# The scores of two jobs in the same columns, attention written as a software pipeline, and more weight buffers, in a two-layer memory-attention and GLU kernel

## Chip, core and metric

The kernel runs on one core of a Trainium2 chip. The metric is the device time of one execution in microseconds (us). Engines are named as in the profile: PE multiplies matrices (PEld is its weight load), DVE and ACT work on vectors, POOL does small things, and the queue of SP issues the loads.

## The reference, cut

Two layers, each an attention block A and a gated feed-forward block B, with the same weights in both layers. A is a recurrence: 64 segments of 32 rows, each preceded by 8 memory rows, which are the first 8 output rows of the segment before.

```python
for s in range(n_seg):                       # 64 segments of 32 rows
    h = concat([mem, x[:, 32*s:32*s+32]])    # 40 rows of 512
    q, k, v = h@Wq, h@Wk, h@Wv               # 32 heads of 128
    p = softmax(where(mask, q@k.T * scale, -1e9))
    o = (p @ v) @ Wo
    mem = o[:, :8]; outs.append(o[:, 8:])
# x = x + A(layernorm(x)); x = x + B(layernorm(x)); the same two again
# B: (sigmoid(x@Wg) * (x@Wu)) @ Wd, inner width 1792
```

## The kernel before

Both layers run interleaved: in step t, job 0 is segment t of layer one and job 1 is segment t-6 of layer two. A step with both jobs has 2 x 40 = 80 columns; 58 of the 70 steps are such. The 32 heads go in groups of 6, 6, 6, 6, 4 and 4. The feed-forward blocks (128 rows each, one for each layer in four steps) are written between the steps. The kernel builder turns the program text into a fixed instruction order for each engine. It may move an instruction ahead of earlier ones when it expects it to be ready first, and text order is its priority. A matmul that waits then holds up the ones behind it: the prediction shows three such waits, of 0.17 to 0.30 us, in front of Q/K matmuls that start only after them.

```python
# first half of a step, for each group g of heads
for u0 in range(0, gsz, 3):                 # units of 3 heads
    # Q and K of 3 heads: 24 matmuls into pj     (L237)
    # ACT copies pj to qku                       (L98)
    # per head one score matmul of 80 columns    (L255)
    nc.tensor.matmul(o_ap, lhsT=qku[:, i, 0, :], rhs=rhs, start=True, stop=True)
for j in jobs:                              # two mask additions (L261)
    nc.vector.tensor_tensor(out=st[pj_, hs], in0=s_all[pj_, hs, L*j:L*j+L], in1=maskb..., op=ALU.add)
# DVE max, subtract; ACT exp; DVE sum, reciprocal, multiply per job (L275)
# PE transposes the probabilities into pt_ps (L287), DVE copies them to ptsb (L99)
# second half, for each group
#   V matmuls (L299), ACT copy; PV matmuls (L305), ACT copy; output projection (L315)
# ... cut ...
self.gpool = ctx.enter_context(tc.tile_pool(name="gp", bufs=2))   # gate and up tiles, 256 KB each
self.dpool = ctx.enter_context(tc.tile_pool(name="dp", bufs=2))   # down tiles, 256 KB each
```

PSUM, the memory that the matmuls write to, has one bank for scores, one for the transposed probabilities, one for PV, one for the projection, one for everything of the feed-forward (`misc`), and three that Q/K and V share (`pj`).

Of the kernel before, what the change touches and what calls it, by code (L numbers as in the profile page):

```python
# [8 lines left out]
BF16 = mybir.dt.bfloat16  # L9
F32 = mybir.dt.float32  # L10
ACTF = mybir.ActivationFunctionType
ALU = mybir.AluOpType
# [3 lines left out]
P = 128  # L16
MEM = 8
SEG = 32
L = MEM + SEG
JOFF = 64  # L20
LW = JOFF + L
# [6 lines left out]
def fview(base, dims):  # L28
    return bass.AP(tensor=base.tensor, offset=base.offset, ap=[tuple(base.ap[0])] + [tuple(d) for d in dims])


class Kern:
# [103 lines left out]
    def _setup_pools(self):  # L136
        ctx, tc, nc = self.ctx, self.tc, self.nc
# [20 lines left out]
        nc.sync.dma_start(out=self.maskb[JOFF:LW, :], in_=self.maskb[0:L, :])  # L158
        self.hT = cpool.tile([P, R, DC, LWP], BF16, name="hT_all")
        nc.vector.memset(self.hT[:], 0.0)  # L160
        self.qku = [cpool.tile([P, 3, 2, P], BF16, name=f"qku{i}") for i in range(3)]
        for t_ in self.qku:
            nc.gpsimd.memset(t_[:], 0.0)
        self.qku_i = 0
# [21 lines left out]
        self.xpool = ctx.enter_context(tc.tile_pool(name="xp", bufs=1))  # L186
        self.bpool = ctx.enter_context(tc.tile_pool(name="bp", bufs=2))
        self.spool = ctx.enter_context(tc.tile_pool(name="sp_small", bufs=4))
        self.gpool = ctx.enter_context(tc.tile_pool(name="gp", bufs=2))
        self.dpool = ctx.enter_context(tc.tile_pool(name="dp", bufs=2))  # L190
        self.oxT = {}
        self.xblk = {}

    def emit_step(self, t):
        nc = self.nc
# [6 lines left out]
        j0 = jobs[0]  # L202
# [10 lines left out]
        def mv(c):  # L213
            if both:
                return fview(hT[:, c, 0:1], [(JOFF, 2), (1, L)])
            return hT[:, c, JOFF * j0:JOFF * j0 + L]
# [1 line left out]
        wo_ps = self.wo_ps  # L218
        first_wo = True
        HGm = self.HG  # L220
        s_all = self.s_ps[:, 0:HGm * 2 * L].rearrange("p (h k) -> p h k", h=HGm)
        pt_all = self.pt_ps[:, 0:HGm * 2 * L].rearrange("p (h k) -> p h k", k=2 * L)
        for g, (h0, gsz) in enumerate(self.groups):
            hs = slice(0, gsz)
            for u0 in range(0, gsz, 3):
                nh = min(3, gsz - u0)
                pq = self.next_pj()
                qku = self.qku[self.qku_i % len(self.qku)]
                self.qku_i += 1
                for i in range(nh):  # L230
                    h = h0 + u0 + i
                    for qk, W in ((0, self.wq), (1, self.wk)):
                        o_ap = pq[:, (2 * i + qk) * ncol:(2 * i + qk + 1) * ncol]
                        if both:
                            o_ap = o_ap.rearrange("p (a b) -> p a b", a=2)
                        for c in range(DC):
                            self.mark("qk_mm", nc.tensor.matmul(o_ap, lhsT=W[:, c, h * P:(h + 1) * P], rhs=mv(c),  # L237
                                                                start=(c == 0), stop=(c == DC - 1)), g)
                src = pq[:, 0:2 * nh * ncol]
                if both:  # L240
                    dst = fview(qku[:, 0, 0, 0:1], [(P, 2 * nh), (JOFF, 2), (1, L)])
                    src = src.rearrange("p (m a b) -> p m a b", a=2, b=L)
                else:
                    dst = fview(qku[:, 0, 0, JOFF * j0:JOFF * j0 + 1], [(P, 2 * nh), (1, L)])
                    src = src.rearrange("p (m b) -> p m b", b=L)
                self.mark("qk_ev", self.evac(dst, src, prefer="act"), g)
                for i in range(nh):
                    hl = u0 + i
                    if both:
                        rhs = fview(qku[:, i, 1, 0:1], [(JOFF, 2), (1, L)])  # L250
                        o_ap = s_all[:, hl, :].rearrange("p (a b) -> p a b", a=2)
                    else:
                        rhs = qku[:, i, 1, JOFF * j0:JOFF * j0 + L]
                        o_ap = s_all[:, hl, L * j0:L * j0 + L]
                    self.mark("s_mm", nc.tensor.matmul(o_ap, lhsT=qku[:, i, 0, :], rhs=rhs, start=True, stop=True), g)  # L255
            st, pb = self.st[g % 2], self.pb[g % 2]
            mx, sm, rs = self.mx[g % 2], self.sm[g % 2], self.rs[g % 2]
            for j in jobs:
                pj_ = slice(0, JOFF) if j == 0 else slice(JOFF, LW)
                npj_ = JOFF if j == 0 else L  # L260
                self.mark("sm_mask", nc.vector.tensor_tensor(  # L261
                    out=st[pj_, hs], in0=s_all[pj_, hs, L * j:L * j + L],
                    in1=self.maskb[pj_, :].unsqueeze(1).to_broadcast([npj_, gsz, L]), op=ALU.add), g)
            self.mark("sm_max", nc.vector.tensor_reduce(out=mx[pr, hs], in_=st[pr, hs], axis=AX.X, op=ALU.max), g)
            self.mark("sm_sub", nc.vector.tensor_tensor(  # L265
                out=st[pr, hs], in0=st[pr, hs],
                in1=mx[pr, hs].unsqueeze(2).to_broadcast([npart, gsz, L]), op=ALU.subtract), g)
            self.mark("sm_exp", nc.scalar.activation(out=st[pr, hs], in_=st[pr, hs], func=ACTF.Exp,  # L268
                                                     scale=self.scale), g)
            self.mark("sm_sum", nc.vector.tensor_reduce(out=sm[pr, hs], in_=st[pr, hs], axis=AX.X, op=ALU.add), g)  # L270
            self.mark("sm_rcp", nc.vector.reciprocal(out=rs[pr, hs], in_=sm[pr, hs]), g)
            for j in jobs:
                pj_ = slice(0, JOFF) if j == 0 else slice(JOFF, LW)
                npj_ = JOFF if j == 0 else L
                self.mark("sm_mul", nc.vector.tensor_tensor(  # L275
                    out=pb[pj_, hs, JOFF * j:JOFF * j + L], in0=st[pj_, hs],
                    in1=rs[pj_, hs].unsqueeze(2).to_broadcast([npj_, gsz, L]), op=ALU.mult), g)
            if both:
                idn = fview(self.ident[:, 0:1], [(JOFF, 2), (1, L)])
            else:  # L280
                idn = self.ident[:, JOFF * j0:JOFF * j0 + L]
            cb = 0 if both else L * j0
            for hl in range(gsz):
                o_ap = pt_all[:, hl, cb:cb + ncol]
                if both:
                    o_ap = o_ap.rearrange("p (a b) -> p a b", a=2)
                self.mark("t_mm", nc.tensor.matmul(o_ap, lhsT=pb[:, hl, :], rhs=idn, start=True, stop=True), g)  # L287
            ptsb = self.ptsb[g]
            self.mark("pt_ev", self.evac(ptsb[:, hs, cb:cb + ncol], pt_all[:, hs, cb:cb + ncol], prefer="dve"), g)
        for g, (h0, gsz) in enumerate(self.groups):  # L290
            vsb = self.vsb[g % 2]
            ptsb = self.ptsb[g]
            hs = slice(0, gsz)
            vun = 3 if gsz % 3 == 0 else 4
            for n in range(gsz // vun):
                pv = self.next_pj()
                col0 = (h0 + vun * n) * P
                for c in range(DC):
                    self.mark("v_mm", nc.tensor.matmul(pv[0:LWP, 0:vun * P], lhsT=hT[:, c, :],  # L299
                                                       rhs=self.wv[:, c, col0:col0 + vun * P],  # L300
                                                       start=(c == 0), stop=(c == DC - 1)), g)
                self.mark("v_ev", self.evac(vsb[pr, vun * n * P:(vun * n + vun) * P], pv[pr, 0:vun * P], prefer="act"), g)
            cb = 0 if both else L * j0
            for hl in range(gsz):
                self.mark("pv_mm", nc.tensor.matmul(  # L305
                    self.ot_ps[:, hl * ncol:(hl + 1) * ncol], lhsT=vsb[:, hl * P:(hl + 1) * P],
                    rhs=ptsb[:, hl, cb:cb + ncol], start=True, stop=True), g)
            otsb = self.otsb[g % 2]
            self.mark("ot_ev", self.evac(otsb[:, hs, 0:ncol],
                                         self.ot_ps[:, 0:gsz * ncol].rearrange("p (h q) -> p h q", q=ncol),  # L310
                                         prefer="act"), g)
            for hl in range(gsz):
                h = h0 + hl
                for c in range(DC):
                    self.mark("wo_mm", nc.tensor.matmul(  # L315
                        wo_ps[:, c * ncol:(c + 1) * ncol], lhsT=self.wo[:, h, c * P:(c + 1) * P],
                        rhs=otsb[:, hl, 0:ncol], start=first_wo, stop=(h == H - 1 and c == DC - 1),
                        skip_group_check=True), g)
                    first_wo = False
        wo3 = wo_ps[:, 0:DC * ncol].rearrange("p (c n) -> p c n", c=DC)  # L320
        nslot = self.hT[:, (t + 1) % R]
        wj = [(idx, j) for idx, j in enumerate(jobs) if (t - j * LAG) + 1 < NSEG]
# [245 lines left out]
```

## Time and profile before

| | before |
|---|---|
| median of 15 runs | 2635.65 us (2632.59 to 2643.47) |
| profiled span, granted clock | 2637.4 us, 0.984 |
| PE busy / streaming at its best | 2276.6 us / 1945 us |
| steps of a block of four | 49.7, 32.9, 36.2, 35.1 us |

"Streaming at its best" is the time that all matmuls would take with no gap between them; the prediction works it out. What the starts hold beyond it is called excess below, and each bit of it is put on the matmul that started late. A step's length is the distance from one copy of the memory rows to the next; the four are averages over the steady part. The lines of the profile stand in the prediction. Line numbers differ between kernels, so each fence below says what is what.

### The profile page before, as it was taken

What the parts mean: (1) busy time and instruction counts of PE and PEld (TensorE: products, weight loads), DVE (VectorE), ACT (ScalarE), POOL (GpSimd) and SP (SyncE); (2) the same over time, 40 slices, a digit from 0 to 9 for tenths busy, and PEclk for the clock granted to TensorE, in tenths of its full rate; (3) what the DMA queues carried; (4) which work ended last, traced back from release to release, by engine and by line L of the source; (5) the groups of instructions that cost most, each with busy time, mean ns of one, the idle gap of its engine ahead of it and who ended that gap; (6) DMA issues with size and microseconds to landing.
All of it is one profiled execution on the core that took longest, in us unless ns stands there. A gap on an engine that the chain in (4) does not pass through costs nothing.

```text
span 2637.4 us, 91952 instructions
## 1 busy us (share of the span) xinstructions
PE 2276.6 (86%) x40820; PEld 1808.3 (69%) x40820; DVE 1463.4 (55%) x4297; ACT 1231.4 (47%) x2829; POOL 50.1 (2%) x94
## 2 busy tenths in 40 slices
PE   5988888888888888888888888888888888888896
PEld 4767676676766667667676767667676776667674
DVE  3545654564565566556555645655565565465452
ACT  2544454444444444444444444444444444444452
POOL 0000000000000000000000000000000000000000
PEclk8999999999999999999999999999999999999997
DMA  8030203132131312213131321313132131313223
GB/s 288 3 88 4 86 18 112 48 90 84 40 108 48 111 48 84 88 38 112 48 112 47 90 85 37 109 48 113 47 89 84 42 102 48 113 44 87 86 59 93
DMA packets 314705, 203.08 MB, mean 77 GB/s; under 512 B 11706, under 2 KB 313794, under 8 KB 314306
## 3 DMA queue, kind: packets, MB, share of 16 engines
q1 hardware_dynamic: 313538, 195.10, 25.1%
q8 instruction: 319, 5.23, 0.8%
q0 software_dynamic: 768, 2.10, 0.2%
q14 instruction: 80, 0.66, 0.1%
HBM read 195.04 MB, written 2.10 MB: 75 GB/s over the span
## 4 chain that ended last, share of the span: by engine, by line
PE 36%; DVE 32%; DMA 15%; ACT 10%; issue 5%; POOL 1%; ACTq 0%; SPq 0%; POOLq 0%; DVEq 0%
PE pj L299 8%; DMA wd<-in_B_w_down_dram 8%; DVE pb L275 7%; PE wo_ps L315 7%; DMA wu<-in_B_w_up_dram 6%; DVE st L261 6%; DVE ptsb L99 5%; PE misc_ps L426 5%; PE pt_ps L287 4%; PE pj L237 3%; ACT qku L98 3%; PE misc_ps L462 3%; ACT vsb L98 3%; DVE sm L270 3%; PE s_ps L255 3%
## 5 line engine op out<-in xcount | busy, mean ns | idle before, releaser
L237 PE MATMUL pj<-hT_all,wk_sb 128*128 128x80 bf16 (+1 forms) x8960 | 690.8, 199 | 0.0
L237 PE MATMUL pj<-hT_all,wq_sb 128*128 128x80 bf16 (+1 forms) x8960 | 662.8, 199 | 12.3 <-DVE hT_all L324 5.7
L299 PE MATMUL pj<-wv_sb,hT_all 128*104 128x384 bf16 (+1 forms) x2800 | 654.6, 344 | 0.0
L98 ACT CAST qku<-pj 128x480 bf16<-128x480 f32 (+1 forms) x840 | 394.9, 483 | 400.0 <-PE pj L237 393.1
L237 PEld LDWEIGHTS <-wq_sb 128*128 128x128 bf16 x8960 | 470.4, 100 | 24.1 <-issue 19.0
L98 ACT CAST vsb<-pj 104x384 bf16<-104x384 f32 (+4 forms) x700 | 347.9, 497 | 288.9 <-PE pj L299 282.5
L237 PEld LDWEIGHTS <-wk_sb 128*128 128x128 bf16 x8960 | 478.8, 100 | 2.2 <-issue 0.6
L315 PEld LDWEIGHTS <-wo_sb 128*128 128x128 bf16 x8960 | 368.9, 99 | 119.8 <-issue 89.6
L315 PE MATMUL wo_ps<-otsb,wo_sb 128*128 128x80 bf16 (+1 forms) x8960 | 397.9, 198 | 19.5 <-ACT otsb L98 13.4
L261 DVE TENSOR_TENSOR st<-s_ps,maskb 64x240 f32<-64x240 f32 (+3 forms) x768 | 287.7, 375 | 193.1 <-PE s_ps L255 176.8
L299 PEld LDWEIGHTS <-hT_all 128*104 128x104 bf16 x2800 | 301.5, 128 | 52.1 <-issue 0.2
L98 ACT CAST otsb<-ot_ps 128x480 bf16<-128x480 f32 (+3 forms) x420 | 202.7, 483 | 201.2 <-PE ot_ps L305 200.2
L275 DVE TENSOR_TENSOR pb<-st,rs 64x240 bf16<-64x240 f32 (+3 forms) x768 | 286.4, 373 | 14.7
L255 PE MATMUL s_ps<-qku 128*128 128x80 bf16 (+1 forms) x2240 | 201.1, 199 | 72.2 <-DVE st L261 37.0
L99 DVE CAST ptsb<-pt_ps 128x480 bf16<-128x480 f32 (+3 forms) x420 | 233.6, 556 | 41.4 <-PE pt_ps L287 32.4
L268 ACT ACTIVATE st<-st 104x240 f32<-104x240 f32 (+5 forms) x420 | 160.5, 382 | 151.9 <-DVE st L265 147.9
L255 PEld LDWEIGHTS <-qku 128*128 128x128 bf16 x2240 | 139.4, 98 | 131.9 <-ACT qku L98 63.0
L305 PEld LDWEIGHTS <-vsb 128*128 128x128 bf16 x2240 | 134.4, 99 | 128.9 <-ACT vsb L98 99.4
L287 PE MATMUL pt_ps<-ident,pb 128*128 128x80 bf16 (+1 forms) x2240 | 148.0, 200 | 73.6 <-DVE pb L275 52.3
L305 PE MATMUL ot_ps<-ptsb,vsb 128*128 128x80 bf16 (+1 forms) x2240 | 190.9, 199 | 21.3 <-ACT vsb L98 12.3
L287 PEld LDWEIGHTS <-pb 128*128 128x128 bf16 x2240 | 100.9, 99 | 133.6 <-DVE pb L275 120.9
L426 PE MATMUL misc_ps<-xnT,wg 128*128 128x128 bf16 x1752 | 171.6, 221 | 23.8 <-DMA wg<-in_B_w_gate_dram 10.0
(70 smaller groups left out, 1684.3 us busy)
## 6 DMA issues: line engine op xcount, KB each, us to landing
wg<-in_B_w_gate_dram SPq DMA_DIRECT2D x224, 256.0 KB, 3.1
wu<-in_B_w_up_dram SPq DMA_DIRECT2D x224, 256.0 KB, 3.7
wd<-in_B_w_down_dram SPq DMA_DIRECT2D x224, 256.0 KB, 2.8
wq_sb<-in_A_Wq_dram SPq DMA_DIRECT2D x4, 768.0 KB, 8.3
wk_sb<-in_A_Wk_dram SPq DMA_DIRECT2D x4, 768.0 KB, 9.2
wv_sb<-in_A_Wv_dram SPq DMA_DIRECT2D x4, 768.0 KB, 11.7
wo_sb<-in_A_Wo_dram SPq DMA_DIRECT2D x4, 768.0 KB, 10.8
x<-in_A_x_dram SPq DMA_DIRECT2D x16, 128.0 KB, 3.4
```

Of the source, the lines that this page charges most:

```text
L98: return nc.scalar.copy(out=out, in_=in_)
L99: return nc.vector.tensor_copy(out=out, in_=in_)
L237: self.mark("qk_mm", nc.tensor.matmul(o_ap, lhsT=W[:, c, h * P:(h + 1) * P], rhs=mv(c), start=(c == 0), stop=(c == DC - 1)), g)
L255: self.mark("s_mm", nc.tensor.matmul(o_ap, lhsT=qku[:, i, 0, :], rhs=rhs, start=True, stop=True), g)
L261: self.mark("sm_mask", nc.vector.tensor_tensor(out=st[pj_, hs], in0=s_all[pj_, hs, L * j:L * j + L], in1=self.maskb[pj_, :].unsqueeze(1).t ...
L268: self.mark("sm_exp", nc.scalar.activation(out=st[pr, hs], in_=st[pr, hs], func=ACTF.Exp, scale=self.scale), g)
L275: self.mark("sm_mul", nc.vector.tensor_tensor(out=pb[pj_, hs, JOFF * j:JOFF * j + L], in0=st[pj_, hs], in1=rs[pj_, hs].unsqueeze(2).to_bro ...
L287: self.mark("t_mm", nc.tensor.matmul(o_ap, lhsT=pb[:, hl, :], rhs=idn, start=True, stop=True), g)
L299: self.mark("v_mm", nc.tensor.matmul(pv[0:LWP, 0:vun * P], lhsT=hT[:, c, :], rhs=self.wv[:, c, col0:col0 + vun * P], start=(c == 0), stop= ...
L305: self.mark("pv_mm", nc.tensor.matmul(self.ot_ps[:, hl * ncol:(hl + 1) * ncol], lhsT=vsb[:, hl * P:(hl + 1) * P], rhs=ptsb[:, hl, cb:cb + ...
L315: self.mark("wo_mm", nc.tensor.matmul(wo_ps[:, c * ncol:(c + 1) * ncol], lhsT=self.wo[:, h, c * P:(c + 1) * P], rhs=otsb[:, hl, 0:ncol], s ...
L426: nc.tensor.matmul(gu[:, 2 * i + k, :], lhsT=W[:, c, i * P:(i + 1) * P], rhs=xnT[:, c, :], start=(c == 0), stop=(c == DC - 1))
```

## The change

Its intent: shorten the softmax chain, keep PE from standing in front of something that has only just been asked for, and let weight loads run further ahead. Cut to its core:

```diff
-        self.qku = [cpool.tile([P, 3, 2, P], BF16, ...
+        self.qku = [cpool.tile([P, 3, 4, P], BF16, ...      # q and k apart for each job, zeros elsewhere
-        ... name="gp", bufs=2     ... name="dp", bufs=2
+        ... name="gp", bufs=3     ... name="dp", bufs=4
-                    nc.tensor.matmul(o_ap, lhsT=qku[:, i, 0, :], rhs=rhs, start=True, stop=True)
+                for idx, j in enumerate(jobs):              # both jobs into the same 40 columns
+                    nc.tensor.matmul(s_all[:, hl, :], lhsT=qku[:, i, j, :],
+                        rhs=qku[:, i, 2 + j, JOFF*j:JOFF*j+L], start=(idx == 0), stop=(idx == len(jobs)-1))
-            for j in jobs: ... tensor_tensor(... maskb ...)
+            one tensor_tensor(... maskb ...) over the rows of both jobs
+        for ui, (g, h0, gsz, u0, nh) in enumerate(units):
+            qku = emit_qk(g, h0, gsz, u0, nh)
+            if pending is not None:
+                emit_scores(...)                             # of the unit before
+                if ...: emit_softmax(...); tps.append((ui + 3, pg, pgsz))
+            while tps and tps[0][0] <= ui: emit_tp(...)      # transposes three units later
+        emit_v(*grp[0])
+        if tps: emit_tp(...)                                 # transposes still to come
+        for k in range(ng):
+            if k + 1 < ng: emit_v(*grp[k + 1])               # V one group ahead
+            if tps: emit_tp(...)
+            emit_pv(*grp[k])
+            if k >= 1: emit_wo(*grp[k - 1])                  # projection one group behind
```

More of the change, by code (lines that the diff above doesn't have):

```diff
@@ L160, in _setup_pools @@
         nc.vector.memset(self.hT[:], 0.0)
-        self.qku = [cpool.tile([P, 3, 2, P], BF16, name=f"qku{i}") for i in range(3)]
+        self.qku = [cpool.tile([P, 3, 4, P], BF16, name=f"qku{i}") for i in range(3)]
         for t_ in self.qku:
@@ L188, in _setup_pools @@
         self.spool = ctx.enter_context(tc.tile_pool(name="sp_small", bufs=4))
-        self.gpool = ctx.enter_context(tc.tile_pool(name="gp", bufs=2))
-        self.dpool = ctx.enter_context(tc.tile_pool(name="dp", bufs=2))
+        self.gpool = ctx.enter_context(tc.tile_pool(name="gp", bufs=3))
+        self.dpool = ctx.enter_context(tc.tile_pool(name="dp", bufs=4))
         self.oxT = {}
@@ L220, in emit_step @@
         HGm = self.HG
-        s_all = self.s_ps[:, 0:HGm * 2 * L].rearrange("p (h k) -> p h k", h=HGm)
+        s_all = self.s_ps[:, 0:HGm * L].rearrange("p (h k) -> p h k", h=HGm)
         pt_all = self.pt_ps[:, 0:HGm * 2 * L].rearrange("p (h k) -> p h k", k=2 * L)
+        units = []
         for g, (h0, gsz) in enumerate(self.groups):
-            hs = slice(0, gsz)
-            for u0 in range(0, gsz, 3):
-                nh = min(3, gsz - u0)
-                pq = self.next_pj()
-                qku = self.qku[self.qku_i % len(self.qku)]
-                self.qku_i += 1
-                for i in range(nh):
-                    h = h0 + u0 + i
-                    for qk, W in ((0, self.wq), (1, self.wk)):
-                        o_ap = pq[:, (2 * i + qk) * ncol:(2 * i + qk + 1) * ncol]
-                        if both:
-                            o_ap = o_ap.rearrange("p (a b) -> p a b", a=2)
-                        for c in range(DC):
-                            self.mark("qk_mm", nc.tensor.matmul(o_ap, lhsT=W[:, c, h * P:(h + 1) * P], rhs=mv(c),
-                                                                start=(c == 0), stop=(c == DC - 1)), g)
-                src = pq[:, 0:2 * nh * ncol]
-                if both:
-                    dst = fview(qku[:, 0, 0, 0:1], [(P, 2 * nh), (JOFF, 2), (1, L)])
-                    src = src.rearrange("p (m a b) -> p m a b", a=2, b=L)
-                else:
-                    dst = fview(qku[:, 0, 0, JOFF * j0:JOFF * j0 + 1], [(P, 2 * nh), (1, L)])
-                    src = src.rearrange("p (m b) -> p m b", b=L)
-                self.mark("qk_ev", self.evac(dst, src, prefer="act"), g)
-                for i in range(nh):
-                    hl = u0 + i
-                    if both:
-                        rhs = fview(qku[:, i, 1, 0:1], [(JOFF, 2), (1, L)])
-                        o_ap = s_all[:, hl, :].rearrange("p (a b) -> p a b", a=2)
-                    else:
-                        rhs = qku[:, i, 1, JOFF * j0:JOFF * j0 + L]
-                        o_ap = s_all[:, hl, L * j0:L * j0 + L]
-                    self.mark("s_mm", nc.tensor.matmul(o_ap, lhsT=qku[:, i, 0, :], rhs=rhs, start=True, stop=True), g)
@@ new lines, in emit_step, with emit_qk @@
+            for u0 in range(0, gsz, 3):
+                units.append((g, h0, gsz, u0, min(3, gsz - u0)))
+        def emit_qk(g, h0, gsz, u0, nh):
+            pq = self.next_pj()
+            qku = self.qku[self.qku_i % len(self.qku)]
+            self.qku_i += 1
+            for i in range(nh):
+                h = h0 + u0 + i
+                for qk, W in ((0, self.wq), (1, self.wk)):
+                    o_ap = pq[:, (2 * i + qk) * ncol:(2 * i + qk + 1) * ncol]
+                    if both:
+                        o_ap = o_ap.rearrange("p (a b) -> p a b", a=2)
+                    for c in range(DC):
+                        self.mark("qk_mm", nc.tensor.matmul(o_ap, lhsT=W[:, c, h * P:(h + 1) * P], rhs=mv(c),
+                                                            start=(c == 0), stop=(c == DC - 1)), g)
+            src = pq[:, 0:2 * nh * ncol]
+            if both:
+                dst = fview(qku[:, 0, 0, 0:1], [(2 * P, 2 * nh), (P + JOFF, 2), (1, L)])
+                src = src.rearrange("p (m a b) -> p m a b", a=2, b=L)
+            else:
+                dst = fview(qku[:, 0, j0, JOFF * j0:JOFF * j0 + 1], [(2 * P, 2 * nh), (1, L)])
+                src = src.rearrange("p (m b) -> p m b", b=L)
+            self.mark("qk_ev", self.evac(dst, src, prefer="act"), g)
+            return qku
@@ L256, in emit_step, with emit_scores, emit_softmax @@
+        def emit_scores(g, u0, nh, qku):
+            for i in range(nh):
+                hl = u0 + i
+                for idx, j in enumerate(jobs):
+                    self.mark("s_mm", nc.tensor.matmul(
+                        s_all[:, hl, :], lhsT=qku[:, i, j, :], rhs=qku[:, i, 2 + j, JOFF * j:JOFF * j + L],
+                        start=(idx == 0), stop=(idx == len(jobs) - 1)), g)
+        def emit_softmax(g, gsz):
+            hs = slice(0, gsz)
             st, pb = self.st[g % 2], self.pb[g % 2]
@@ L257, in emit_step @@
             mx, sm, rs = self.mx[g % 2], self.sm[g % 2], self.rs[g % 2]
-            for j in jobs:
-                pj_ = slice(0, JOFF) if j == 0 else slice(JOFF, LW)
-                npj_ = JOFF if j == 0 else L
-                self.mark("sm_mask", nc.vector.tensor_tensor(
-                    out=st[pj_, hs], in0=s_all[pj_, hs, L * j:L * j + L],
-                    in1=self.maskb[pj_, :].unsqueeze(1).to_broadcast([npj_, gsz, L]), op=ALU.add), g)
+            self.mark("sm_mask", nc.vector.tensor_tensor(
+                out=st[pr, hs], in0=s_all[pr, hs],
+                in1=self.maskb[pr, :].unsqueeze(1).to_broadcast([npart, gsz, L]), op=ALU.add), g)
@@ L277, in emit_step, with emit_tp @@
                     in1=rs[pj_, hs].unsqueeze(2).to_broadcast([npj_, gsz, L]), op=ALU.mult), g)
+        def emit_tp(g, gsz):
+            hs = slice(0, gsz)
+            pb = self.pb[g % 2]
             if both:
@@ L289, in emit_step, with emit_wo, emit_v @@
             self.mark("pt_ev", self.evac(ptsb[:, hs, cb:cb + ncol], pt_all[:, hs, cb:cb + ncol], prefer="dve"), g)
-        for g, (h0, gsz) in enumerate(self.groups):
+        pending = None
+        tps = []
+        for ui, (g, h0, gsz, u0, nh) in enumerate(units):
+            qku = emit_qk(g, h0, gsz, u0, nh)
+            if pending is not None:
+                pg, pgsz, pu0, pnh, pq_ = pending
+                emit_scores(pg, pu0, pnh, pq_)
+                if pu0 + pnh == pgsz:
+                    emit_softmax(pg, pgsz)
+                    tps.append((ui + 3, pg, pgsz))
+            while tps and tps[0][0] <= ui:
+                emit_tp(*tps.pop(0)[1:])
+            pending = (g, gsz, u0, nh, qku)
+        pg, pgsz, pu0, pnh, pq_ = pending
+        emit_scores(pg, pu0, pnh, pq_)
+        emit_softmax(pg, pgsz)
+        tps.append((0, pg, pgsz))
+        def emit_wo(g, h0, gsz):
+            nonlocal first_wo
+            otsb = self.otsb[g % 2]
+            for hl in range(gsz):
+                h = h0 + hl
+                for c in range(DC):
+                    self.mark("wo_mm", nc.tensor.matmul(
+                        wo_ps[:, c * ncol:(c + 1) * ncol], lhsT=self.wo[:, h, c * P:(c + 1) * P],
+                        rhs=otsb[:, hl, 0:ncol], start=first_wo, stop=(h == H - 1 and c == DC - 1),
+                        skip_group_check=True), g)
+                    first_wo = False
+        def emit_v(g, h0, gsz):
             vsb = self.vsb[g % 2]
-            ptsb = self.ptsb[g]
-            hs = slice(0, gsz)
             vun = 3 if gsz % 3 == 0 else 4
@@ L302, in emit_step, with emit_pv @@
                 self.mark("v_ev", self.evac(vsb[pr, vun * n * P:(vun * n + vun) * P], pv[pr, 0:vun * P], prefer="act"), g)
+        def emit_pv(g, h0, gsz):
+            vsb = self.vsb[g % 2]
+            ptsb = self.ptsb[g]
+            hs = slice(0, gsz)
             cb = 0 if both else L * j0
@@ L311, in emit_step @@
                                          prefer="act"), g)
-            for hl in range(gsz):
-                h = h0 + hl
-                for c in range(DC):
-                    self.mark("wo_mm", nc.tensor.matmul(
-                        wo_ps[:, c * ncol:(c + 1) * ncol], lhsT=self.wo[:, h, c * P:(c + 1) * P],
-                        rhs=otsb[:, hl, 0:ncol], start=first_wo, stop=(h == H - 1 and c == DC - 1),
-                        skip_group_check=True), g)
-                    first_wo = False
+        grp = [(g, h0, gsz) for g, (h0, gsz) in enumerate(self.groups)]
+        ng = len(grp)
+        emit_v(*grp[0])
+        if tps:
+            emit_tp(*tps.pop(0)[1:])
+        for k in range(ng):
+            if k + 1 < ng:
+                emit_v(*grp[k + 1])
+            if tps:
+                emit_tp(*tps.pop(0)[1:])
+            emit_pv(*grp[k])
+            if k >= 1:
+                emit_wo(*grp[k - 1])
+        emit_wo(*grp[ng - 1])
         wo3 = wo_ps[:, 0:DC * ncol].rearrange("p (c n) -> p c n", c=DC)
```

## The prediction

> **What bounds the kernel now.** First the page: its engine line, then the chain that ended last.
>
> ```profile
> PE 2276.6 (86%) x40820; PEld 1808.3 (69%) x40820; DVE 1463.4 (55%) x4297; ACT 1231.4 (47%) x2829; POOL 50.1 (2%) x94
> ...
> PE 36%; DVE 32%; DMA 15%; ACT 10%; issue 5%; POOL 1%; ACTq 0%; SPq 0%; POOLq 0%; DVEq 0%
> PE pj L299 8%; DMA wd<-in_B_w_down_dram 8%; DVE pb L275 7%; PE wo_ps L315 7%; DMA wu<-in_B_w_up_dram 6%; DVE st L261 6%; DVE ptsb L99 5%; PE misc_ps L426 5%; PE pt_ps L287 4%; PE pj L237 3%; ACT qku L98 3%; PE misc_ps L462 3%; ACT vsb L98 3%; DVE sm L270 3%; PE s_ps L255 3%
> ```
>
> PE is the fullest engine, yet only 36% of the chain is PE: it keeps being handed to DVE, DMA and ACT. So PE is busy but not streaming. To size that I used the matmul start times in the trace. In the last part of the run, where a step has 40 columns, four matmuls with their weight loads start every 0.10 us (25 ns each); in the middle, with 80 columns, four take 0.14 us (36 ns); eight of 384 columns take 1.48 us with one tail (about 163 ns each). These are max(25, N/2.4 + 2.5) ns. Summed over all recorded matmuls this gives 1945 us of pure streaming. From the first matmul to the last the spacing holds 683 us more than that. I put each excess on the matmul that came late:
>
> - scores (L255) 151; probability transposes (L287) 128; PV (L305) 63; output projection (L315) 68
> - gate/up (L426) 90; down (L462) 85
> - layer-norm transposes (L358) 57; Q, K, V and the rest about 41.
>
> The list of PE's waits names who was late (its figures are smaller, since each break also has a modelled tail of some 0.17 us counted as busy):
>
> ```profile
> PE misc_ps L462 <- DMA wd<-in_B_w_down_dram: 59.0, 89, 3.3
> PE pt_ps L287 <- DVE pb L275: 52.3, 186, 1.2
> PE s_ps L255 <- DVE st L261: 37.0, 134, 0.4
> ...
> PE s_ps L255 <- ACT qku L98: 21.3, 114, 0.4
> PE misc_ps L426 <- DMA wu<-in_B_w_up_dram: 19.5, 37, 1.9
> ```
>
> Then the timeline of one step. The copy of the memory rows into the next step's input (L324) ends a step; here two are 32.9 us apart.
>
> ```profile
> 1230.49 0.22 DVE L324 CAST hT_all<-wo_ps 128x64 bf16<-128x64 f32 x1 [1.33 <-PE wo_ps L315]
> ...
> 1234.97 0.82 DVE L261 TENSOR_TENSOR st<-s_ps,maskb 64x240 f32<-64x240 f32 x2 [1.06 <-PE s_ps L255]
> 1235.83 0.40 DVE L264 TENSOR_REDUCE mx<-st 104x6 f32<-104x240 f32 x1
> ...
> 1255.26 0.49 DVE L99 CAST ptsb<-pt_ps 128x320 bf16<-128x320 f32 x1 [0.41 <-PE pt_ps L287]
> 1263.38 0.22 DVE L324 CAST hT_all<-wo_ps 128x64 bf16<-128x64 f32 x1 [7.64 <-PE wo_ps L315]
> ```
>
> From 1235.0 to 1255.8 DVE works almost without a gap: the six softmax groups set the pace there. Afterwards DVE idles 7.6 us while PE works off V, PV and the output projection. PE's ideal for this step type is 26 us, so 7 us are lost, 4.5 of them in front of scores and transposes. PE's own order in the first half:
>
> ```profile
> 1237.22 0.28 PE L255 MATMUL s_ps<-qku 128*128 128x80 bf16 x3 [0.17 <-ACT qku L98]
> 1238.74 0.27 PE L255 MATMUL s_ps<-qku 128*128 128x80 bf16 x3 [0.20 <-DVE st L261]
> 1239.99 0.39 PE L287 MATMUL pt_ps<-ident,pb 128*128 128x80 bf16 x6 [0.30 <-DVE pb L275]
> ```
>
> Each stands in front of Q/K matmuls that were ready. The instruction order on PE is fixed when the kernel is built, and it puts these a little before their input arrives. Between copies, the four steps of a block last 49.7, 32.9, 36.2 and 35.1 us on average in the steady part (PE ideal 37.0, 26.1, 26.5, 26.8). The long one carries a whole feed-forward block, and its chain alternates between weight load and matmul:
>
> ```profile
> 1212.65 3.49 DMA wd<-in_B_w_down_dram
> 1216.14 0.04 issue
> 1216.18 0.59 PE misc_ps L462 x2
> ...
> 1216.81 3.14 DMA wd<-in_B_w_down_dram
> ```
>
> With two buffers each 256 KB load starts only when an older tile is used up.
>
> **What the Trainium skill says.** "TensorE: Matmul & The Clock Gate", section "Back-to-back issue gap", gives N/2.4 + 2.5 ns for a warm clock and a floor near 25 ns for small N, and warns that weight loads can raise it. The trace agrees with the formula at 80 and 40 columns and shows no weight-load penalty (granted clock 0.984). "PSUM — Partial Sum Buffer", section "PSUM bank collisions raise a hardware error", says writer and reader of one bank must be kept apart; that fits the scores waiting 37.0 us for the mask addition that empties the one score bank. "Perfetto Trace Analysis", section "Identifying Performance Opportunities", says repeated gaps can mean too few buffers; the weight-load chain above is such a case. The same page, section "Optimizing Scalar/DVE Operations", speaks of a fixed cost per DVE instruction and of gain from grouping; here the mask addition takes 395 ns on 64 partitions and 410 on 40, so two cost twice one.
>
> **The change, part by part.**
>
> 1. *Scores of two jobs into the same 40 columns, as two accumulating matmuls.* Steps with both jobs have 1856 score matmuls of 80 columns; they become 3712 of 40: from 36 to 2 x 25 ns each, (50 - 36) x 1856 = +26 us, all on PE. The ACT copy keeps its 480 columns per unit; only its target is spread more widely.
> 2. *One mask addition instead of two.* 768 become 420: 348 fewer at about 375 ns = 130 us less DVE busy time. Per step the starts show 0.43 us for four groups and 0.33 for two, some 2.4 us off the 20.8 us that DVE paces. This is not added to the PE gains; it is one reason for the smaller scores and transposes terms below.
> 3. *Scores one unit later, behind the next unit's Q/K.* 24 matmuls x 36 ns = 0.86 us lie between, against a 0.56 us copy plus latency. The ACT waits should nearly go. Waits for the one score bank shrink but stay, for DVE still paces it. 151 -> 75: -76 us.
> 4. *Transposes three units later.* About 3 us more work ahead of them, but a softmax takes 5 us with its neighbours (1235.0 to 1239.9). The built order still places them by expected readiness. 128 -> 100: -28 us.
> 5. *V of the next group ahead of PV, and the output projection one group later.* V of the next group is 8 x 163 ns = 1.3 us against copies of about 0.5 us, and PV is followed by an older group's 24 x 36 = 0.86 us. PV 63 -> 25, output projection 68 -> 25: -81 us.
> 6. *Three gate/up buffers, four down buffers.* Four of seven down tiles can be resident before they are needed; the rest are asked for earlier. Down 85 -> 40. Gate/up waits also for its one bank and the tanh chain, so 90 -> 65. Together -70 us.
>
> Layer norms and Q/K/V stay at 98. Sum: 26 - 76 - 28 - 81 - 70 = -229 us, or 2637 - 229 = 2408 us. The sizes of the remainders are my choice.
>
> **Rivals.**
>
> *The waits only change place.* DVE still has to finish six softmaxes, and an in-order PE then stands at the transposes instead of the scores. For it: 20.8 us without a gap on DVE, 52 us of waits at transposes. Against: PE's ideal (26 to 37 us a step) is longer than the DVE part even now. Then only the merged mask (up to 2.4 us x 58 steps = 139, half of it hidden) and the loads count, less 26: about 2540.
>
> *The schedule is already as overlapped as this,* and only the extra 26 us of PE and larger strides are felt: 2650. For it: the built order already interleaves V, FFN and Q/K. Against: the 683 us of excess are real gaps.
>
> *The loads are hidden anyway or slow each other,* as three or four in flight share the DMA engines: part 6 gives nothing, 2480. Against: DMA engines are busy some 25% on average.
>
> *Everything overlaps:* DVE no longer paces, excess falls to about 300: 2637 - 683 + 300 + 26 = 2280.
>
> **Range and chances.** Four of the parts pull the same way and only one costs, with a known small cost. The main doubt is how much the DVE rival keeps. I predict 2408 us, with 2290 to 2540 for 8 in 10. Faster by over 2% 0.90, within 2% 0.06, slower by over 2% 0.04.
>
> **What would show it.** Score matmuls near 4096 at 40 columns; mask additions 420 and DVE busy near 1330 us; PE's waits for the qku copy, for vsb and for otsb almost gone; waits at transposes for pb still there; waits for wd at most half of 59 us; ordinary steps near 30 us instead of 33 to 36, and the long one near 45. I am wrong if the transposes' waits grow to what scores, PV and projection lost (first rival), or if DMA keeps its 15% of the chain.

## The result, and the profile after

The median of 8 runs is 2403.35 us (2399.8 to 2409.67). The ratio to the kernel before is 0.9116 (95% interval 0.9103 to 0.9128). A ratio here is the mean time of one kernel's runs over that of the other's in the same rounds, so it isn't quite the ratio of the medians.

The page of the kernel after: engine line and chain.

```profile
PE 2154.7 (90%) x42676; PEld 1830.7 (76%) x42676; DVE 1308.4 (55%) x3949; ACT 1218.4 (51%) x2829; POOL 52.1 (2%) x94
...
PE 41%; DVE 37%; ACT 8%; DMA 6%; issue 5%; SPq 2%; POOL 1%; ACTq 0%; POOLq 0%; DVEq 0%
```

DMA's share of the chain fell from 15% to 6%, ACT's from 10% to 8%. PE has 122 us less busy time although it runs 1856 matmuls more. That is no contradiction: each break in its stream adds a modelled tail, and there are fewer breaks (807 instead of 1465, counted in the two traces). DVE lost 155 us of busy time, most of it the 348 mask additions.

PE's waits in the kernel after (L293 transposes, L509 down, L405 layer-norm transposes, L255 scores):

```profile
PE pt_ps L293 <- DVE pb L277: 60.4, 228, 1.6
PE misc_ps L509 <- DMA wd<-in_B_w_down_dram: 47.2, 49, 2.1
...
PE s_ps L255 <- DVE st L263: 8.7, 50, 0.3
PE s_ps L255 <- ACT qku L98: 8.2, 34, 0.4
```

The two waits of the scores fell from 37.0 and 21.3 us to 8.7 and 8.2. The wait of the transposes for pb rose from 52.3 to 60.4. Gate and up hardly wait for a load any more (0.9 us is left, of 29.5), while the down matmuls still do.

The matching step on DVE (L371 is the copy of the memory rows, L263 the mask addition):

```profile
1116.71 0.23 DVE L371 CAST hT_all<-wo_ps 128x64 bf16<-128x64 f32 x1 [6.95 <-PE wo_ps L321]
...
1122.17 0.41 DVE L263 TENSOR_TENSOR st<-s_ps,maskb 104x240 f32<-104x240 f32 x1 [0.85 <-PE s_ps L255]
...
1139.11 0.49 DVE L99 CAST ptsb<-pt_ps 128x320 bf16<-128x320 f32 x1 [0.41 <-PE pt_ps L293]
1147.38 0.23 DVE L371 CAST hT_all<-wo_ps 128x64 bf16<-128x64 f32 x1 [7.78 <-PE wo_ps L321]
```

The softmax part takes 1139.60 - 1122.17 = 17.4 us instead of 20.8, and the step 30.7 us instead of 32.9. DVE then waits 7.8 us for the projection, much as before.

The excess, worked out as in the prediction, in us:

| in front of | before | after |
|---|---|---|
| scores | 151 | 58 |
| transposes | 128 | 113 |
| PV | 63 | 20 |
| output projection | 68 | 15 |
| gate/up | 90 | 60 |
| down | 85 | 59 |
| layer-norm transposes | 57 | 61 |
| Q, K, V and the rest | 41 | 31 |
| sum | 683 | 417 |
| PE at its best | 1945 | 1971 |

Excess fell by 266 us and the work rose by 26, 240 net, against 238 us between the two profiled spans. A small part of this excess is a slower clock and no wait: the granted clock was 0.984 before and 0.994 after, since the stretches at half clock add up to 85 us before and 30 us after. Some 21 us of the 683 and 8 us of the 417 come from slower matmuls there, an estimate from the starts in these stretches. The steps last 45.1, 30.7, 32.8 and 32.1 us instead of 49.7, 32.9, 36.2 and 35.1.

### The profile page after: what moved, and what is told of

Its sections match the earlier page's. It is cut to its first block, busy times and chain, and to the rows that moved or that the text cites. A ratio compares the mean times of both kernels' runs of the same rounds, so it can differ in the third digit from the quotient of the medians.

```text
span 2399.6 us, 95290 instructions
## 1 busy us (share of the span) xinstructions
PE 2154.7 (90%) x42676; PEld 1830.7 (76%) x42676; DVE 1308.4 (55%) x3949; ACT 1218.4 (51%) x2829; POOL 52.1 (2%) x94
## 4 chain that ended last, share of the span: by engine, by line
PE 41%; DVE 37%; ACT 8%; DMA 6%; issue 5%; SPq 2%; POOL 1%; ACTq 0%; POOLq 0%; DVEq 0%
PE pj L334 10%; PE wo_ps L321 9%; DVE pb L277 9%; PE misc_ps L473 7%; PE pj L239 6%; DVE ptsb L99 6%; DMA wd<-in_B_w_down_dram 5%; DVE sm L272 4%; DVE mx L266 4%; DVE st L263 4%; DVE hff L479 3%; PE misc_ps L509 3%; DVE st L267 2%; PE pt_ps L293 2%; PE ot_ps L345 2%
## 5 line engine op out<-in xcount | busy, mean ns | idle before, releaser
L239 PE MATMUL pj<-hT_all,wk_sb 128*128 128x80 bf16 (+1 forms) x8960 | 658.5, 198 | 2.4 <-issue 2.4
L239 PE MATMUL pj<-hT_all,wq_sb 128*128 128x80 bf16 (+1 forms) x8960 | 646.6, 197 | 5.6 <-DVE hT_all L376 1.4
L334 PE MATMUL pj<-wv_sb,hT_all 128*104 128x384 bf16 (+1 forms) x2800 | 595.9, 341 | 0.9 <-DMA wv_sb<-in_A_Wv_dram 0.9
L239 PEld LDWEIGHTS <-wq_sb 128*128 128x128 bf16 x8960 | 455.3, 98 | 14.0 <-issue 10.0
L321 PE MATMUL wo_ps<-otsb,wo_sb 128*128 128x80 bf16 (+1 forms) x8960 | 382.1, 198 | 3.1 <-ACT otsb L98 2.8
L321 PEld LDWEIGHTS <-wo_sb 128*128 128x128 bf16 x8960 | 335.9, 99 | 10.3 <-issue 3.1
L99 DVE CAST ptsb<-pt_ps 128x480 bf16<-128x480 f32 (+3 forms) x420 | 233.7, 556 | 32.8 <-PE pt_ps L293 28.1
L371 DVE CAST hT_all<-wo_ps 128x64 bf16<-128x64 f32 x57 | 12.8, 224 | 432.0 <-PE wo_ps L321 432.0
L255 PE MATMUL s_ps<-qku 128*128 128x40 bf16 x4096 | 229.0, 180 | 19.8 <-DVE st L263 8.7
L263 DVE TENSOR_TENSOR st<-s_ps,maskb 104x240 f32<-104x240 f32 (+5 forms) x420 | 154.9, 369 | 117.0 <-PE s_ps L255 112.6
L255 PEld LDWEIGHTS <-qku 128*128 128x128 bf16 x4096 | 183.9, 97 | 45.2 <-issue 20.9
L293 PE MATMUL pt_ps<-ident,pb 128*128 128x80 bf16 (+1 forms) x2240 | 155.0, 200 | 64.1 <-DVE pb L277 60.4
L293 PEld LDWEIGHTS <-pb 128*128 128x128 bf16 x2240 | 102.0, 99 | 125.3 <-DVE pb L277 119.3
L473 PE MATMUL misc_ps<-xnT,wg 128*128 128x128 bf16 x1752 | 169.9, 219 | 25.2 <-DVE hff L479 7.8
L478 ACT ACTIVATE th<-misc_ps 128x256 f32<-128x256 f32 x219 | 83.9, 383 | 198.0 <-PE misc_ps L473 185.0
```

The lines of the kernel that those rows point to most:

```text
L99: return nc.vector.tensor_copy(out=out, in_=in_)
L239: self.mark("qk_mm", nc.tensor.matmul(o_ap, lhsT=W[:, c, h * P:(h + 1) * P], rhs=mv(c), start=(c == 0), stop=(c == DC - 1)), g)
L255: self.mark("s_mm", nc.tensor.matmul(s_all[:, hl, :], lhsT=qku[:, i, j, :], rhs=qku[:, i, 2 + j, JOFF * j:JOFF * j + L], start=(idx == 0), ...
L263: self.mark("sm_mask", nc.vector.tensor_tensor(out=st[pr, hs], in0=s_all[pr, hs], in1=self.maskb[pr, :].unsqueeze(1).to_broadcast([npart, ...
L293: self.mark("t_mm", nc.tensor.matmul(o_ap, lhsT=pb[:, hl, :], rhs=idn, start=True, stop=True), g)
L321: self.mark("wo_mm", nc.tensor.matmul(wo_ps[:, c * ncol:(c + 1) * ncol], lhsT=self.wo[:, h, c * P:(c + 1) * P], rhs=otsb[:, hl, 0:ncol], s ...
```

## The experiments

Twelve kernels ran; each was profiled and then timed in three rounds against the kernel before. All gave correct results. "Worth" is the difference of two ratios times the 2640 us of the kernel before; by the intervals it is uncertain by some 4 to 9 us.

In eight of the twelve traces, 32 to 93 of the 448 down matmuls have no record, though their weight loads have one (the trace with the old buffers holds 42583 matmuls and 42676 weight loads). Each such hole would count as 0.216 us of excess, 7 to 20 us in a trace. The figures of excess below leave the holes out, each missing matmul being placed behind its weight load. In the lists of waits up to 7 us of those for wd can still be such holes.

### Parts alone, and the buffers taken out

**Layout only**: the kernel before with the new score layout and the one mask addition.

```diff
 # on the kernel before
-  one 80-column score matmul per head; two mask additions
+  two accumulating 40-column matmuls per head; one mask addition
```

> The kernel before with only the new score layout: two accumulating 40-column score matmuls per head and one mask addition; old order, old buffers. Theory A (the order of the instructions on PE is the main lever, the layout a small one): PE pays 26 us, the shorter DVE chain gives back some 50, so about 2610 us. Rival B (DVE paces, and the merged mask is what counted): up to 139 us less DVE on the path less 26, so about 2520 us.

Measured 2615.19 us, ratio 0.9905 (0.9888 to 0.9921): worth 25 us. Theory A's number. The transposes' excess fell from 128 to 83, but the scores' rose from 151 to 159 and PE paid for its 1856 extra matmuls.

**Order only**: the kernel after with the old layout and the old buffers.

```diff
 # on the kernel after
-  accumulating 40-column scores, one mask addition, bufs 3 and 4
+  one 80-column score matmul, two mask additions, bufs 2 and 2
```

> The kernel after with the old score layout (one 80-column matmul per head, two mask additions) and the old two and two buffers: only the order is new. Theory A: scores, PV and output projection lose most of their waits, about 93 + 42 + 53 = 188 us in the traces of before and after, so about 2460 us. Rival B: the waits only move to the probability transposes, 2580 us or more.

Measured 2552.02 us, ratio 0.9661 (0.9645 to 0.9677): worth 89 us, half of theory A's figure. PV and projection gave what they give in the whole change (131 to 38 us of excess), the scores about half (151 to 104, against 58). The rest came back elsewhere, as the waits of PE show (L299 transposes, L515 down, L260 scores):

```profile
PE pt_ps L299 <- DVE pb L283: 80.0, 213, 1.6
PE misc_ps L515 <- DMA wd<-in_B_w_down_dram: 77.3, 94, 2.8
PE s_ps L260 <- DVE st L269: 53.1, 128, 0.7
```

All three are longer than in the kernel before (52.3, 59.0 and 37.0): part of what the order had freed went into waits for DVE and for loads. Rival B was half right here.

**Buffers only**: the kernel before with three and four buffers.

```diff
-  name="gp", bufs=2    name="dp", bufs=2
+  name="gp", bufs=3    name="dp", bufs=4
```

> The kernel before with three gate/up and four down buffers and nothing else. Theory A: the excess in front of gate/up and down matmuls falls as it did in the whole change (30 + 26 us), so about 2580 us. Rival C (the loads are hidden, or take longer when more of them fly together): within 15 us of the kernel before, 2635.

Measured 2575.14 us, ratio 0.9752 (0.9737 to 0.9766): worth 65 us. Gate/up fell from 90 to 52 us of excess, down from 85 to 60. Rival C falls.

**The kernel after with the old buffers.**

```diff
-  name="gp", bufs=3    name="dp", bufs=4
+  name="gp", bufs=2    name="dp", bufs=2
```

> The kernel after with the buffers back at two and two. Theory A: the buffers are worth as much here as alone, about 56 us, so about 2460 us. Rival C: within 15 us of the kernel after, 2403 to 2418. If it loses much more than 56, a faster attention part leaves less work behind which a load can hide.

Measured 2499.53 us, ratio 0.9464 (0.945 to 0.9478): the buffers are worth 92 us here, more than the 65 alone. The excess in front of gate/up and down is 115 + 103 us, above the 90 + 85 of the kernel before. The steps tell where: 49.7, 30.7, 33.7 and 32.1 us. Two short ones are as short as in the kernel after, the third is 0.9 us longer, but the long one, which holds a whole feed-forward block, is back at the 49.7 us of the kernel before, on average (single ones vary from 47.6 to 52.1). So with two buffers the new attention gained nothing in that step, and the waits for loads grew instead. They are, over the whole run (L509 down, L473 gate and up):

```profile
PE misc_ps L509 <- DMA wd<-in_B_w_down_dram: 80.5, 94, 2.7
...
PE misc_ps L473 <- DMA wu<-in_B_w_up_dram: 29.5, 60, 1.6
...
PE misc_ps L473 <- DMA wg<-in_B_w_gate_dram: 13.8, 25, 1.5
```

So the parts are worth some 180 us if added up alone and 233 together (2640 x 0.0884). Order and layout together give 142 us (this kernel against before), some 27 more than alone, and the buffers some 26 more on top of them.

### The order taken apart

**Scores at once**: each unit's scores right behind its own Q/K.

```diff
             qku = emit_qk(g, h0, gsz, u0, nh)
+            pending = (g, gsz, u0, nh, qku)                  # its own scores now
             if pending is not None:
                 ... emit_scores ...
```

> The kernel after, but each unit's scores are written right behind its own Q/K again (V, projection, transposes, layout, buffers as after). If the one-unit delay is what took the scores' excess from 151 to 58 us, it comes back: about +90, 2495 us. If the builder's reordering finds the same order by itself, or the merged mask did it, it stays near 2403.

Measured 2460.84 us, ratio 0.931 (0.929 to 0.9329): 51 us lost. The scores' excess came back in full and more (170), but the transposes' fell to 78, so only half reached the time. The waits (L255 scores, L293 transposes):

```profile
PE s_ps L255 <- ACT qku L98: 41.0, 236, 0.6
PE pt_ps L293 <- DVE pb L277: 26.0, 112, 1.2
```

A PE that has stood in front of scores comes later to the transposes, and more often finds their input ready: the wait for pb fell from 60.4 to 26.0 us.

**Old second half**: V, PV and projection of one group after another. The edit also moves the transposes that the kernel after writes among them to before the first V.

```diff
-            if k + 1 < ng: emit_v(*grp[k + 1])
-            emit_pv(*grp[k])
-            if k >= 1: emit_wo(*grp[k - 1])
+            emit_v(*grp[k]); emit_pv(*grp[k]); emit_wo(*grp[k])
-            if tps: emit_tp(...)             # one before the loop, one in each turn
+        while tps: emit_tp(...)              # now all before the first V
```

> The kernel after, but V, PV and output projection of one group follow each other as before. If that order is what took PV and projection from 131 to 35 us of excess, it comes back: about +95, 2500 us. If the waits only move elsewhere, near 2420.

Measured 2512.19 us, ratio 0.9497 (0.9472 to 0.9521): 101 us lost. PV and projection are at 61 + 71 = 132 us, the 131 of the kernel before; nothing else moved much, and the transposes moved with it kept theirs (108 instead of 113). This is the cleanest of the levers: hardly any other excess fell in return.

**Transposes at once**, right behind each softmax.

```diff
-                    tps.append((ui + 3, pg, pgsz))
+                    tps.append((ui, pg, pgsz))
```

> The kernel after, but each group's probability transposes are written right behind its softmax, not three units later. I expect little, for the builder places them when it thinks them ready either way and their excess hardly moved (128 to 113 us): 2400 to 2420. If the delay counts, they lose some 0.3 us for each of 420 groups: 2500 and more.

Measured 2421.49 us, ratio 0.9164 (0.9143 to 0.9186): 13 us lost, 0.5%. The transposes' excess rose from 113 to 147. A small lever, as expected, though the time is just above the 2400 to 2420 us that were forecast: gate/up gave 12 us back (60 to 48).

### DVE and PE on the path

**Two masks**: the new layout, but two mask additions again.

```diff
-  one tensor_tensor over rows 0 to 103
+  for j in jobs: one tensor_tensor over that job's rows
```

> The kernel after with the mask added by two instructions again, one per job, on the same new score layout: 348 more DVE instructions, PE work the same. If DVE paces the first half of a step, nearly all of their 0.31 to 0.43 us starts to count where nothing else is late: order alone against order plus layout with old buffers differed by 52 us though the latter had 26 us more PE work, so about +80, 2483 us. If PE is now the bound and DVE has slack, +15 at most, 2418.

Measured 2497.74 us, ratio 0.9446 (0.9429 to 0.9463): 87 us lost, 0.25 us for each of the 348 instructions. Most of it is at the transposes (181 us of excess instead of 113), the rest at the scores (75 instead of 58) and the feed-forward. Its largest wait of PE (L296 transposes), and then its chain by engine:

```profile
PE pt_ps L296 <- DVE pb L280: 102.3, 254, 1.6
```

```profile
DVE 46%; PE 35%; ACT 6%; DMA 6%; issue 5%; POOL 1%; SPq 1%; ACTq 0%; POOLq 0%; DVEq 0%
```

With those instructions DVE holds 46% of the chain, more than PE.

**No maximum**: if adding 348 DVE instructions costs 87 us, what does removing 840 give?

```diff
-            tensor_reduce(out=mx, in_=st, op=ALU.max)
-            tensor_tensor(out=st, in0=st, in1=mx, op=ALU.subtract)
```

> The kernel after without subtracting the row maximum before the exponential (mathematically the same softmax, safe only for scores as small as these): 840 DVE instructions fewer, PE's and ACT's work unchanged. The 348 extra mask additions cost 0.25 us each. If DVE still paces the first half, the waits in front of scores and transposes (58 + 113 us) mostly go: -100 to -150, about 2280 us. If DVE has slack by now, 2390 or more.

Measured 2416.96 us, ratio 0.9147 (0.9115 to 0.9178), so no gain at all: by medians it is 0.6% slower, by ratios the intervals overlap. Its profiled execution had a lower granted clock (0.987 against 0.994), which by the same estimate as above costs some 11 us; that leaves no gain either. My theory that a shorter DVE chain would shorten the step falls. The engine line of the page, and then the same short step on DVE (L263 mask addition, L367 copy of the memory rows):

```profile
PE 2154.7 (89%) x42629; PEld 1835.7 (76%) x42676; DVE 1085.2 (45%) x3109; ACT 1218.6 (50%) x2829; POOL 51.1 (2%) x94
```

```profile
1130.17 0.41 DVE L263 TENSOR_TENSOR st<-s_ps,maskb 104x240 f32<-104x240 f32 x1 [0.86 <-PE s_ps L255]
...
1145.38 0.49 DVE L99 CAST ptsb<-pt_ps 128x320 bf16<-128x320 f32 x1 [0.41 <-PE pt_ps L289]
1155.48 0.23 DVE L367 CAST hT_all<-wo_ps 128x64 bf16<-128x64 f32 x1 [9.61 <-PE wo_ps L317]
```

DVE is busy 223 us less. The softmax part did shrink, to 1145.87 - 1130.17 = 15.7 us from 17.4, but DVE then waits 9.6 us at the end of the step instead of 7.8. Yet the steps last 46.4, 30.8, 32.9 and 32.1 us against 45.1, 30.7, 32.8 and 32.1: the three shorter ones are equal to 0.1 us, and the 1.3 us in the long one are the feed-forward's. Scores and transposes together keep their excess, 87 + 78 = 165 us against 171, but stand for other things (L289 transposes, L255 scores):

```profile
PE pt_ps L289 <- DVE ptsb L99: 36.0, 44, 0.8
PE s_ps L255 <- DVE st L263: 32.2, 66, 0.8
```

The transposes no longer wait for pb but for the copy that empties their one bank, the scores for the mask addition that empties theirs. The builder made a new PE order around the shorter chain, and it comes out at the same length. The last transposes of the step, in the kernel after and then here:

```profile
1138.75 0.32 PE L293 MATMUL pt_ps<-ident,pb 128*128 128x80 bf16 x4 [0.17 <-DVE pb L277]
```

```profile
1145.02 0.32 PE L289 MATMUL pt_ps<-ident,pb 128*128 128x80 bf16 x4
```

In the kernel after they start 22.0 us into the step and have 24 V, 12 PV and 13 projection matmuls ahead of them; here it is 20.3 us, with 17, 6 and none. So the time that DVE gave up was not turned into fewer waits: the transposes moved forward, other work moved behind them, and PE has 3.8 and 3.9 us of excess in the two steps. What the shorter chain would give in the old order was not tested.

**Extra scores**: one more score matmul per head, overwritten by the next.

```diff
+                matmul(s_all[:, hl, :], lhsT=qku[:, i, jobs[0], :], rhs=..., start=True, stop=True)
                 for idx, j in enumerate(jobs): ...
```

> The kernel after with one more 40-column score matmul per head, which the next one overwrites: 2240 more matmuls of 25 ns, 56 us of PE and nothing else. It tells whether the 26 us that the layout adds to PE are paid in full. If PE's stream sets the time: +56, 2459 us. If part of it falls into time in which PE waits for DVE anyway: +20 to +35, 2430 us. The second is my guess.

Measured 2487.6 us, ratio 0.9418 (0.9389 to 0.9447): 80 us lost for 56 us of matmuls. I had guessed that part of it would hide; none does. The excess grew as well, from 417 to 447 us, mostly at the scores (58 to 84). So work added to PE at this place is on the path in full, as the work added to DVE was with two masks. Why the excess grew too stays open: the order was built anew.

### A better version

**Shared ring**: the same 20 KB per partition, as one ring of ten tiles for all three weights.

```diff
-  gpool bufs=3 (tags wg, wu)    dpool bufs=4 (tag wd)
+  gpool bufs=10, one tag for wg, wu and wd
```

> The kernel after with the same 20 KB per partition for feed-forward weights, but as one ring of ten tiles for gate, up and down instead of three, three and four. All seven down tiles can then be on their way before the first is used. If the 59 us in front of down matmuls are lack of buffers: about -35, 2368 us. If they are the builder's too early placing, no change, 2403.

Measured 2346.82 us, ratio 0.8886 (0.8863 to 0.8909): 61 us faster than the kernel after. The down matmuls' excess fell from 59 to 3 us. The largest waits for loads that are left to the gate/up and down matmuls (L472, L508) in the list of PE's waits, and then the load issues (count, size, us from issue to landing):

```profile
PE misc_ps L472 <- DMA wd<-in_B_w_down_dram: 1.6, 5, 0.3
PE misc_ps L508 <- DMA wd<-in_B_w_down_dram: 0.8, 4, 0.3
```

```profile
wg<-in_B_w_gate_dram SPq DMA_DIRECT2D x224, 256.0 KB, 3.9
wu<-in_B_w_up_dram SPq DMA_DIRECT2D x224, 256.0 KB, 4.1
wd<-in_B_w_down_dram SPq DMA_DIRECT2D x224, 256.0 KB, 4.3
```

The loads are slower than those of the kernel before, 4.3 us against 2.8 from issue to landing of a down tile, perhaps because more of them fly together, which wasn't tested; but hardly a matmul waits for them. The long step is down to 43.5 us.

**No maximum and shared ring.**

```diff
+  both edits
```

> Both of the last: no row maximum and the shared ring. If the two act on different waits their gains add: about -155, 2248 us. As buffers and order gained more together than apart, it may be somewhat more.

Measured 2343.65 us, ratio 0.8873 (0.885 to 0.8896), against 0.8886 for the ring alone: the same. It confirms that the shorter DVE chain gives nothing, without the loads in the way (three shorter steps 30.8, 31.2 and 32.1 us against 30.7, 31.2 and 32.2). The ring with the maximum kept is the version to use; leaving the maximum out buys nothing and is safe only for small scores.

## Why the prediction was right

The number (2408 against 2403.35 us) and its direction held; its parts held unevenly. That the total is within 5 us is partly luck: PV and projection gave 15 us more than forecast and the buffers 14 us less, and the remainders were a choice. Neither sign of being wrong came: the wait for pb grew only from 52.3 to 60.4 us, and DMA's share of the chain fell from 15% to 6%. Two of its rivals' sums are loose: the terms named for the first give 2637 - 70 - 70 + 26 = 2523 us, not 2540, and 26 us more would be 2663, not 2650. Nothing rests on them.

- *Extra PE work, +26 us.* PE at its best rose by 26. That it lies wholly on the path is supported by the extra scores, of which nothing hid.
- *PV and projection, -81 us.* 131 to 35, so -96; and undoing that part alone cost 101 us. The step as argued, mis-sized by 15.
- *Scores and transposes, -104 us.* The trace shows 279 to 171, -108, though split otherwise (-93 and -15 instead of -76 and -28). What I did not see is how this term comes about. Taking scores and transposes together, neither half alone does it:

| | old scores order | delayed scores |
|---|---|---|
| two masks | 279 (before) | 246 (order only), 256 (two masks) |
| one mask | 242 (layout only), 248 (scores at once) | 171 (after), 156 (old buffers) |

  Either half saves 23 to 37 us, both save 108. I had credited the merged mask only as "one reason" for smaller remainders; undoing it costs 87 us. The rival "the waits only change place" is what happens with one half: delay the scores, and PE meets the same slow chain at the transposes; shorten the chain, and PE stands at the scores.
- *Buffers, -70 us.* In the two traces -30 for gate/up and -26 for down. The term mis-sized is "Down 85 -> 40": it went to 59. Four buffers for seven tiles were not enough; the ring brought 3. And the wait for down tiles in the list was to be at most half of 59 us; it was 47.2. What buffers are worth depends on the rest: 65 us alone, 92 on top of order and layout.
- *DVE paces the first half.* In the kernel before, the new layout alone gained 25 us net although PE paid 26 for it, and with two masks the kernel after loses 87, so DVE's work did count there, and more of it still counts in the kernel after. Less of it no longer gains anything, which only the two kernels without the maximum could show.

Two predicted signs held to the number: 420 mask additions and 4096 score matmuls of 40 columns. PE's waits for the copies of V and of PV's output are almost gone (12.3 to 2.4 and 13.4 to 2.8 us), those for the Q/K copy are less so (21.3 to 8.2). DVE's busy time was 1308 us, near the 1330 named; the long step 45.1, near 45; the ordinary ones 30.7 to 32.8, "near 30" only for the shortest. Layer norms were left as they are, and they are (57 to 61).

What stays open: which wait one would have to remove to shorten the 30.7 us step, in which PE's best is 26.6. Taking two DVE instructions per group out did not; the PE order that was built for it has as much excess, in part in other places. That the order is built on expected instead of real times is my reading of these waits, not something a run isolated.

## What to carry to other kernels

On an engine with a fixed order, put independent work between an instruction and the one that produces its input, and do it at every link of the chain at once: here one link alone handed much of its wait to the next. A wait listed against an engine tells who came last, not what a faster engine would give; adding and removing work on it are two different tests, and both are cheap. And size load buffers after the compute is tightened, as one shared ring where tiles are alike: the same memory was worth 61 us more that way. Count the records of a trace before working with their gaps: a missing one looks like a wait.

## What the Trainium skill lacked or had wrong

- "TensorE: Matmul & The Clock Gate", section "Back-to-back issue gap": for streams of weight load and matmul it gives a sustained spacing of about 81 ns at N = 128 and 131 ns at N = 512, besides the formula N/2.4 + 2.5. Here the streams, each matmul with its own weight load, keep to the formula. In the lines below, of the kernel before, four gate/up matmuls of 128 columns take 0.225 us (56 ns each), and three V matmuls of 512 columns last 0.83 us with one modelled end of 0.39, so (0.83 - 0.39)/2 = 0.22 us each.

```profile
1207.05 0.39 PE L426 MATMUL misc_ps<-xnT,wg 128*128 128x128 bf16 x4
1207.28 0.39 PE L426 MATMUL misc_ps<-xnT,wu 128*128 128x128 bf16 x4
1207.50 0.38 PE L287 MATMUL pt_ps<-ident,pb 128*128 128x80 bf16 x6
...
1224.07 0.83 PE L299 MATMUL pj<-wv_sb,hT_all 128*104 128x512 bf16 x3
```

- "Perfetto Trace Analysis", section "Identifying Performance Opportunities": it has one find the gaps on the most-contended engine and what they wait for, and make that finish faster. It lacks that such a wait need not be worth its removal where the instruction order is built anew with the change: 223 us less DVE busy time, on the engine that PE's largest wait named, gave no gain, while 348 DVE instructions more cost 87 us.
- No page read here has that buffers for loads gain in worth as the compute is tightened: 65 us before, 92 us after the rest of the change.
